# Loads that give each partition two neighbouring tokens, in a gated recurrence with an FFN behind it

## The chip, the cores and the metric

The kernel runs on one core of a Trainium2 chip. The core has five engines that run beside each other: TensorE (PE, matrix products; its weight loads are listed as PEld), VectorE (DVE), ScalarE (ACT), GpSimd (POOL) and SyncE (SP, which here only issues transfers). They share an on-chip memory of 128 partitions (SBUF), a smaller one for matmul results (PSUM) and 16 DMA engines. The metric is the device time of one execution in microseconds, and lower is better. The median of three runs of the kernel before is 515.47 us (515.06 to 516.38).

## What is computed

The input is a batch of 4 sequences of 5824 tokens with 256 channels. A gated linear recurrence runs over each sequence, and its output goes through a feed-forward network with a product in the middle.

```python
log_a = c * sigmoid(r_gate) * log(clip(sigmoid(a_param)))   # c = 8
a_t   = exp(log_a)
x_gated = sqrt(max(1 - a_t * a_t, 1e-6)) * sigmoid(i_gate) * x
h = a_t[:, t] * h + x_gated[:, t]      # for t = 0 .. S-1; y[:, t] = h
a, b = y @ w1, y @ w2                  # 256 -> 1024
out = ((a * b) @ w3) @ w_out           # 1024 -> 1024 -> 256
```

## The kernel before

The 23,296 tokens are cut into 47 chunks: two of 256 tokens, 44 of 512, and one of 256 at the end. The recurrence runs along time, so it needs channels on the partitions and tokens along the free dimension, while the inputs lie in DRAM with tokens as rows. Each chunk therefore goes through these steps (the letters are those of the written order):

- `r`, `i`, `x` (`load`, L133): SP loads the three inputs with tokens on the partitions. Chunks in both sets `TURN_R` and `TURN_U` (0 to 4 and 7, `long_rows`) give each partition neighbouring tokens, in one run of 2 or 4 KB. All others give partition p the tokens p, p + 128, p + 256 and p + 384 of the chunk, in runs of 1 KB.
- `R`, `I`: ACT takes tanh of both gates. `p`, `t` (L159, L178): mostly POOL, adds one and multiplies with x.
- `V`, `U`: the results are turned so that channels lie on the partitions. Chunks in `TURN_R` (for V) or `TURN_U` (for U) are turned by TensorE into PSUM (tile `ptr`), all others by a transposing DMA into SBUF (tiles `rt` and `ut`). The turned tile holds the 128 tokens of the first slot, then those of the second, and so on.
- `d` (`decay`, L200): ACT takes the exponential into `a_t`, in order of time. `s` squares it, on POOL, ACT or DVE; `q` takes the root on ACT.
- `g` (`gated`, L224): DVE computes max(n, 1e-3) times the turned gated input, in place in `nrm`. For long rows it walks the PSUM tile with a step of 128 elements, so that `nrm` is in order of time.
- `h` (L249): DVE runs the recurrence as two scans, one for each 128 channels. `y`: POOL casts the state to bfloat16.
- `a`, `b` (L268): TensorE multiplies with `w1` and `w2`. `c` (L282 on DVE, L284 on ACT): the first product is copied out of PSUM. `m` (L296): DVE multiplies it with the second, which it reads from PSUM.
- `D` (L307): TensorE multiplies with the product of `w3` and `w_out`, which is formed once at the start. `e`, `o`: the result is copied out and stored.

The order of all these steps is one list written out by hand (`ORDER`). Each engine works through its own part of that list in order and waits on semaphores for what it needs from the others. The gate steps of a chunk stand several chunks ahead of its FFN steps. Buffers are rings of a fixed length (`RINGS`): 4 one-bank PSUM tiles `po` for the first products, the turns and the results, 2 two-bank tiles `pb` for the second products, 3 `sa` and 3 `g`.

Of the kernel before, what the change touches and what calls it, by code (L numbers as in the profile page):

```python
# [13 lines left out]
ALU = mybir.AluOpType  # L14
# [8 lines left out]
def kernel(  # L23
# [12 lines left out]
    nc = tc.nc  # L36
    P = 128
# [11 lines left out]
    CT = 512  # L49
    sizes = [256, 256] + [CT] * 44 + [256]  # L50
    assert sum(sizes) == NTOK
    NCH = len(sizes)
    starts = [sum(sizes[:c]) for c in range(NCH)]
# [24 lines left out]
    T = {}  # L78
# [27 lines left out]
    def ring(pool, shape, dtype, name, tag):  # L106
        slot = taken[tag] % RINGS[tag]
        taken[tag] += 1
        return pool.tile(shape, dtype, name=name, tag=f"{tag}_{slot}")

    src = {"r": rf, "i": jf, "x": xf}
# [12 lines left out]
    def long_rows(c):  # L124
        return c in TURN_R and c in TURN_U

    def turned(t):
        return t.rearrange("p (j q) -> p q j", q=P)

    def in_time(t):  # L130
        return t.rearrange("p (q j) -> p q j", q=P)

    def load(c, nm):  # L133
        n = sizes[c] // P
        t = ring(loads, [P, 4, D], F32, name=nm + "_t", tag=nm)
        nc.sync.dma_start(  # L136
            out=t[:, :n, :],
            in_=src[nm][starts[c]:starts[c] + sizes[c], :].rearrange("(p n) c -> p n c" if long_rows(c) else "(n p) c -> p n c", p=P))
        T[nm, c] = t

    def tanh_r(c):
# [58 lines left out]
    def decay(c, cb):  # L200
        w = sizes[c]
        if cb == 0:
            T["a", c] = ring(held, [P, NCB, CT], F32, name="a_t", tag="a")
        a, pr = T["a", c][:, cb, :w], T["pr", c][:, cb, :w]
        if long_rows(c):
            a, pr = in_time(a), turned(pr)
        nc.scalar.activation(out=a, in_=pr, func=AF.Exp, scale=la4[:, cb:cb + 1], bias=la4[:, cb:cb + 1])  # L207

    def square(c, cb):
# [14 lines left out]
    def gated(c):  # L224
        w = sizes[c]
        if long_rows(c):
            for cb in range(NCB):
                n = in_time(T["n", c][:, cb, :w])
                nc.vector.scalar_tensor_tensor(out=n, in0=n, scalar=1e-3, in1=turned(T["pu", c][:, cb, :w]),
                                               op0=ALU.max, op1=ALU.mult)  # L230
            return
        nc.vector.scalar_tensor_tensor(  # L232
            out=T["n", c][:, :, :w], in0=T["n", c][:, :, :w], scalar=1e-3,
            in1=T["pu", c][:, :, :w], op0=ALU.max, op1=ALU.mult)

    def scan(c, cb):
        w = sizes[c]
# [179 lines left out]
    def last(c):  # L417
        return c == NCH - 1

    steps = {  # L420
        "r": lambda c: load(c, "r"), "i": lambda c: load(c, "i"), "x": lambda c: load(c, "x"),
        "R": tanh_r, "I": tanh_i, "p": plus, "t": times,
        "V": lambda c: turn_pe(c, "pr", "thr") if c in TURN_R else turn_dma(c, "pr", "thr"),
        "U": lambda c: turn_pe(c, "pu", "u") if c in TURN_U else turn_dma(c, "pu", "u"),
        "d": decay, "s": square, "q": root, "g": gated, "h": scan, "y": cast,
        "a": up_a, "b": up_b,
        "c": copy, "m": product, "D": down,
# [181 lines left out]
```

## Time and profile before

| What | Value |
|---|---|
| Median of three runs | 515.47 us (515.06 to 516.38) |
| Profiled execution | span 513.8 us from the first to the last instruction; no other time is listed for it |
| Granted clock of TensorE | 1.00 |
| DMA packets | 177,281, of these 86,354 under 512 B |
| Loads r, i, x of 512 KB | 44 each, median 5.3, 5.9 and 5.9 us from issue to landing |
| Turns by DMA | 40 of r, 39 of u, median 4.4 us |
| HBM read and written | 78.91 and 23.86 MB |

The page lists the busy time of each engine and its share of the span, a row of digits for each engine (its busy tenths in 40 equal slices of the span), the waits, and groups of instructions by line. In a group, the numbers behind the first bar are the total busy time in us and the mean of one instruction in ns; those behind the second are the idle time of the engine just before these instructions and what ended it. A wait is read as "who, at which line, waited for whom: us in total, times, longest". In the timeline a row begins with its start and its length in us. Several instructions of one kind in a row are merged, so a length can be that of two.

### The profile page before, as it was taken

The numbers are of one execution on the slowest core, as the hardware profiler recorded it, in microseconds if no ns is written. First come the engines' busy times: TensorE is split into PE (matmuls) and PEld (weight loads), VectorE is DVE, ScalarE is ACT, GpSimd is POOL, SyncE is SP. The second block draws the span as 40 slices with busy tenths as digits, with TensorE's granted clock in tenths as the row PEclk, the third lists the DMA queues.
The fourth block names the chain that finished last, engine by engine and source line by source line (L and its number), as shares of the span: only waits on it lengthen the run. The fifth ranks groups of instructions, "written<-read, shape, count | busy, mean of one in ns | idle before, by whom it ended". The sixth has DMA issues, their size and how long they took to land.

```text
span 513.8 us, 9036 instructions
## 1 busy us (share of the span) xinstructions
PE 499.8 (97%) x3267; PEld 314.2 (61%) x3321; DVE 430.6 (84%) x414; ACT 465.5 (91%) x720; POOL 312.9 (61%) x271
## 2 busy tenths in 40 slices
PE   7889999999999999999999999999999999999997
PEld 7658565566565566556656556564566655656566
DVE  5889999999999889978878799888878697959762
ACT  8899999999999999999999999998998979888543
POOL 2583858646637956866595983957646569480200
PEclk9999999999999999999999999999999999999999
DMA  8997999999989998896999996989795995252112
GB/s 299 410 414 255 305 315 285 312 240 316 314 242 269 266 276 261 221 276 201 289 288 310 262 272 191 234 228 246 197 265 132 215 316 170 101 150 76 54 60 103
DMA packets 177281, 123.82 MB, mean 241 GB/s; under 512 B 86354, under 2 KB 172884, under 8 KB 177236
## 3 DMA queue, kind: packets, MB, share of 16 engines
q1 hardware_dynamic: 177232, 123.23, 84.6%
q8 instruction: 26, 0.43, 0.3%
q14 instruction: 19, 0.16, 0.1%
q10 hardware_dynamic: 4, 0.00, 0.0%
HBM read 78.91 MB, written 23.86 MB: 200 GB/s over the span
## 4 chain that ended last, share of the span: by engine, by line
PE 86%; ACT 5%; DMA 4%; issue 2%; DVE 2%; SPq 1%; ACTq 0%; DVEq 0%
PE po L307 29%; PE pb L268 28%; PE pa L268 27%; DMA r_t<-in_r_gate_dram 4%; ACT sa L284 2%; PE pw L378 1%; PE ptr L185 1%; DVE g_t L296 1%; PE ptw L367 1%; ACT ot L284 1%; SPq L136 1%; DVE h_t L249 1%; ACT i_t L154 1%; ACT a_t L207 1%; ACT L154 0%
## 5 line engine op out<-in xcount | busy, mean ns | idle before, releaser
L296 DVE TENSOR_TENSOR g_t<-sa,pb 128x1024 bf16<-128x1024 bf16 (+1 forms) x188 | 219.0, 1181 | 62.0 <-PE pb L268 29.1
L268 PEld LDWEIGHTS <-w_sb 128*128 128x128 bf16 x1504 | 146.3, 98 | 146.8 <-issue 5.5
L284 ACT CAST sa<-pa 128x512 bf16<-128x512 f32 (+1 forms) x339 | 182.4, 588 | 27.6 <-PE pa L268 18.3
L268 PE MATMUL pa<-y_t,w_sb 128*128 128x512 bf16 (+1 forms) x721 | 185.9, 372 | 4.5 <-ACT sa L284 3.5
L268 PE MATMUL pb<-y_t,w_sb 128*128 128x512 bf16 (+1 forms) x729 | 182.5, 372 | 1.5
L307 PE MATMUL po<-wp_sb,g_t 128*128 128x256 bf16 x1456 | 177.7, 273 | 0.4
L307 PEld LDWEIGHTS <-g_t 128*128 128x128 bf16 x1456 | 142.4, 98 | 40.5 <-issue 0.9
L258 POOL CAST y_t<-h_t 128x1024 bf16<-128x1024 f32 (+1 forms) x46 | 51.2, 1112 | 141.2 <-DVE h_t L249 138.8
L178 POOL TENSOR_TENSOR u_t<-i_t,x_t 128x512 bf16<-128x512 f32 (+1 forms) x89 | 120.0, 1365 | 5.5 <-DMA ut<-u_t 2.5
L249 DVE TENSOR_TENSOR_SCAN h_t<-a_t,h_t,nrm 128x512 f32<-128x512 f32 (+1 forms) x92 | 121.0, 1345 | 1.9
L217 POOL TENSOR_TENSOR nrm<-a_t 128x512 f32<-128x512 f32 (+1 forms) x74 | 81.3, 1116 | 12.8 <-ACT a_t L207 9.9
L207 ACT ACTIVATE a_t<-rt,la 128x512 f32<-128x512 bf16 (+1 forms) x80 | 64.2, 821 | 0.0
L159 POOL TENSOR_SCALAR i_t<-i_t 128x1024 f32<-128x1024 f32 (+1 forms) x45 | 53.4, 1189 | 17.6 <-ACT i_t L154 17.6
L284 ACT COPY ot<-po 128x512 f32<-128x512 f32 (+1 forms) x85 | 49.6, 590 | 11.8 <-PE po L307 11.5
L232 DVE SCALAR_TENSOR_TENSOR nrm<-nrm,ut 128x1024 f32<-128x1024 f32 (+1 forms) x39 | 54.4, 1394 | 5.2 <-ACT nrm L221 5.2
L154 ACT ACTIVATE i_t<-i_t 128x1024 f32<-128x1024 f32 (+1 forms) x47 | 49.2, 1049 | 0.1
L221 ACT ACTIVATE nrm<-nrm 128x1024 f32<-128x1024 f32 (+1 forms) x47 | 48.4, 1040 | 0.2
L147 ACT ACTIVATE th_r<-r_t 128x1024 bf16<-128x1024 f32 (+1 forms) x40 | 42.6, 1065 | 0.0
L282 DVE CAST sa<-pa 128x512 bf16<-128x512 f32 (+1 forms) x37 | 21.9, 617 | 1.4 <-PE pa L268 1.1
L221 ACT ACT_TABLE_LOAD x17 | 21.8, 1283 | 0.4
L215 ACT ACTIVATE nrm<-a_t 128x512 f32<-128x512 f32 (+1 forms) x17 | 10.7, 648 | 0.1
L263 PE MATMUL warm<-ident 128*128 128x128 bf16 x128 | 10.2, 247 | 0.0
(57 smaller groups left out, 132.6 us busy)
## 6 DMA issues: line engine op xcount, KB each, us to landing
out_dram<-ot SPq DMA_DIRECT2D x90, 256.0 KB, 3.4
r_t<-in_r_gate_dram SPq DMA_DIRECT2D x44, 512.0 KB, 5.3
i_t<-in_i_gate_dram SPq DMA_DIRECT2D x44, 512.0 KB, 5.9
x_t<-in_x_dram SPq DMA_DIRECT2D x44, 512.0 KB, 5.9
wf<-in_moe_w_dram SPq DMA_DIRECT2D x12, 512.0 KB, 10.1
wf<-in_moe_w_out_dram SPq DMA_DIRECT2D x2, 512.0 KB, 10.5
r_t<-in_r_gate_dram SPq DMA_DIRECT2D x3, 256.0 KB, 2.7
i_t<-in_i_gate_dram SPq DMA_DIRECT2D x3, 256.0 KB, 3.8
```

The source lines that it names most:

```text
L154: nc.scalar.activation(out=t[:, :n, :], in_=t[:, :n, :], func=AF.Tanh, scale=0.5)
L159: (nc.vector if c in DV_PLUS else nc.gpsimd).tensor_scalar(t, t, 1.0, 1.0, op0=ALU.add, op1=ALU.mult)
L178: (nc.vector if (c, half) in DV_HALF else nc.gpsimd).tensor_mul(out=u, in0=t, in1=xt)
L207: nc.scalar.activation(out=a, in_=pr, func=AF.Exp, scale=la4[:, cb:cb + 1], bias=la4[:, cb:cb + 1])
L217: (nc.vector if (c, cb) in DV_SQUARE else nc.gpsimd).tensor_mul(out=n, in0=a, in1=a)
L221: nc.scalar.activation(out=T["n", c][:, :, :w], in_=T["n", c][:, :, :w], func=AF.Sqrt, scale=-1.0, bias=1.0)
L232: nc.vector.scalar_tensor_tensor(out=T["n", c][:, :, :w], in0=T["n", c][:, :, :w], scalar=1e-3, in1=T["pu", c][:, :, :w], op0=ALU.max, op1 ...
L249: nc.vector.tensor_tensor_scan(h[:, cb, :], a[:, cb, :], n[:, cb, :], init, ALU.mult, ALU.add)
L268: nc.tensor.matmul(out=dst[:, :w], lhsT=w_sb[:, cb, m * P:(m + 1) * P], rhs=T["y", c][:, cb, :w], start=(cb == 0), stop=(cb == NCB - 1))
L284: nc.scalar.copy(out=dst, in_=src_ps)
L296: nc.vector.tensor_mul(out=T["g", c][:, 2 * mp:2 * mp + 2, :w], in0=T["sa", c, mp][:, :, :w], in1=T["pb", c, mp][:, :, :w])
L307: nc.tensor.matmul(out=po, lhsT=T["g", c][:, k, j * P:(j + 1) * P], rhs=wp_sb[:, k, :], start=(k == 0), stop=(k == KD - 1), skip_group_che ...
```

## The change

Chunks that are not `long_rows` now give partition p the tokens 2p and 2p + 1 of each 256 tokens, one run of 2 KB, instead of single tokens 128 apart. After the turn, the 128 even tokens of a 256-token block lie in front of its 128 odd ones. Two steps put them back in order of time as they write or walk the float32 tile with a step of two elements: the exponential, which stays one instruction for each 128 channels, and the gated input, which becomes two instructions, one for the even and one for the odd tokens. The scans, the squares and all that follows read tiles in order of time as before. Loads of long rows, and the steps behind them, keep their form.

```diff
+    def run(c):
+        return sizes[c] // P if long_rows(c) else 2
+
+    def paired(t):
+        return t.rearrange("p (h q j) -> p h j q", q=P, j=2)
+
+    def halves(t):
+        return t.rearrange("p (h j q) -> p h j q", q=P, j=2)
+
 ...
         nc.sync.dma_start(
-            out=t[:, :n, :],
-            in_=src[nm][starts[c]:starts[c] + sizes[c], :].rearrange("(p n) c -> p n c" if long_rows(c) else "(n p) c -> p n c", p=P))
+            out=t[:, :n, :].rearrange("p (h j) c -> p h j c", j=run(c)),
+            in_=src[nm][starts[c]:starts[c] + sizes[c], :].rearrange("(h p j) c -> p h j c", p=P, j=run(c)))
 ...
         if long_rows(c):
             a, pr = in_time(a), turned(pr)
+        else:
+            a, pr = paired(a), halves(pr)
         nc.scalar.activation(out=a, in_=pr, func=AF.Exp, scale=la4[:, cb:cb + 1], bias=la4[:, cb:cb + 1])
 ...
-        nc.vector.scalar_tensor_tensor(
-            out=T["n", c][:, :, :w], in0=T["n", c][:, :, :w], scalar=1e-3,
-            in1=T["pu", c][:, :, :w], op0=ALU.max, op1=ALU.mult)
+        for j in range(2):
+            if w == CT:
+                n = T["n", c].rearrange("p cb (x j) -> p j (cb x)", j=2)[:, j].rearrange("p (y q) -> p y q", q=P)
+                pu = T["pu", c].rearrange("p cb (h j q) -> p j (cb h) q", q=P, j=2)[:, j]
+            else:
+                n = T["n", c][:, :, :w].rearrange("p cb (q j) -> p j cb q", j=2)[:, j]
+                pu = T["pu", c][:, :, :w].rearrange("p cb (j q) -> p j cb q", q=P)[:, j]
+            nc.vector.scalar_tensor_tensor(out=n, in0=n, scalar=1e-3, in1=pu, op0=ALU.max, op1=ALU.mult)
```

## The prediction

> **What bounds the kernel now.** I read the page's busy times and slices first, then the waits by engine, then groups by form, then the timeline around single instructions.
>
> ```profile
> PE 499.8 (97%) x3267; PEld 314.2 (61%) x3321; DVE 430.6 (84%) x414; ACT 465.5 (91%) x720; POOL 312.9 (61%) x271
> ...
> PE   7889999999999999999999999999999999999997
> ...
> DVE  5889999999999889978878799888878697959762
> ACT  8899999999999999999999999998998979888543
> ```
>
> A busy PE is not yet PE at its peak, so I compared the starts of neighbouring matmuls: 512 columns take 216 ns and 256 take 109 ns nearly everywhere from 28 us to 511 us. The gaps beyond that are mostly of one matmul's length, the mark of missing records. TensorE sets the end and has perhaps 1 us to give back after the start-up. VectorE and ScalarE run close beside it:
>
> ```profile
> 55.00:100.00 45.00, 44.70 (x294) 27.61 (x298) 43.83 (x47) 44.82 (x65) 32.22 (x30) 1.00 1.12 301
> 250.00:300.00 50.00, 49.74 (x305) 30.13 (x309) 40.88 (x32) 48.92 (x77) 39.37 (x32) 1.00 1.06 285
> ```
>
> (The columns are the stretch, its length, busy us of PE, weight loads, DVE, ACT and POOL, clock, DMA share, GB/s.) ACT is 98 to 99% busy until 350 us; DVE falls from 97% to between 82 and 90%. The waits tell who is late for whom:
>
> ```profile
> PE pa L268 <- ACT sa L284: 3.5, 3, 2.2
> PE ptr L185 <- ACT th_r L145: 2.2, 2, 1.2
> ...
> DVE g_t L296 <- PE pb L268: 29.1, 35, 2.7
> DVE g_t L296 <- ACT sa L284: 19.9, 25, 2.4
> ```
>
> PE hardly waits for anybody, and DVE's largest wait is for PE. So removing work elsewhere gains nothing; adding work costs only where it uses up the lead that DVE and ACT have over PE.
>
> **What the Trainium skill says.** "SBUF — State Buffer", section "SBUF: two separate sides", says that GpSimd shares a port pair with VectorE under an exclusive lock: a VectorE operation with two SBUF inputs and a GpSimd operation that reads SBUF exclude each other for a whole instruction. The trace agrees. The gated input is such an operation:
>
> ```profile
> 181.34 2.50 POOL L178 TENSOR_TENSOR u_t<-i_t,x_t 128x512 bf16<-128x512 f32 x2 [0.98 <-DMA ut<-u_t]
> 182.65 2.28 DVE L232 SCALAR_TENSOR_TENSOR nrm<-nrm,ut 128x1024 f32<-128x1024 f32 x1 [1.24 <-ACT nrm L221]
> ...
> 445.15 3.19 DVE L249 TENSOR_TENSOR_SCAN h_t<-a_t,h_t,nrm 128x512 f32<-128x512 f32 x2
> ...
> 445.57 1.69 POOL L217 TENSOR_TENSOR nrm<-a_t 128x512 f32<-128x512 f32 x1 [0.30 <-ACT a_t L207]
> ```
>
> At 182.65 the gated input took 2.28 us instead of its usual 1.22 because POOL's product had started 0.08 us before it. At 445 two scans follow each other without a gap, and POOL asked in the middle of the first. POOL got the ports between the two, and the second scan took 2.00 us instead of 1.26. This is the pattern that matters below.
>
> "SBUF — State Buffer", section "Specifications (TRN2)", gives 16-byte lines with at least two accesses per line needed for full bandwidth. A step of two float32 is 8 bytes, two accesses per line, so just inside. No instruction of this trace steps through SBUF element by element, so it neither agrees nor disagrees. "VectorE: DVE Perf Modes", section "Walkthrough: the 8-slice pipeline in each mode", says that the one-element-a-cycle mode takes any stride. The gated input runs at that rate: (1222 - 680)/512 = 1.06 ns an element.
>
> **The change, part by part.** All durations are of the profiled execution (span 513.8 us). The median of the runs is 515.47, 1.67 us above that span, and I add differences to the median.
>
> *Loads.* Chunks 5, 6 and 8 to 45 have three loads of 512 KB each, and chunk 46 three of 256 KB. Their 1 KB packets become half as many 2 KB packets. In the packet records a 1 KB packet takes 46 ns and a 2 KB packet 84 ns (medians), so 62,208 x 46 / 16 = 179 us of each DMA engine become 31,104 x 84 / 16 = 163 us, 16 us less. After the start-up only POOL is listed as waiting for a load, three times, 3.1 us in all, and POOL is busy for 61%. The loads of chunks 0 to 4 and 7, which are waited for at the start, keep their form. Worth nothing, then; SP issues as many transfers in the same order.
>
> *Decay.* The 82 Exp instructions of those chunks write float32 with a step of two. Neither their number nor their place changes. The long-row form (strided read from PSUM, contiguous write) took 784 ns against 773 for the contiguous one from the same source, so a strided read costs 1%; a strided write isn't shown. At best it costs nothing; at worst the part that grows with size doubles, which is 2 x (827 - 600) = 454 ns by the rows of 512 and 256 elements, +37 us of ACT. I take zero, by the 16-byte lines.
>
> *Gated input.* One instruction over 1024 becomes two over 512, 41 instructions more on DVE.
>
> ```profile
> L249 DVE TENSOR_TENSOR_SCAN h_t<-a_t,h_t,nrm 128x512 f32<-128x512 f32 x88 | 118.1, 1372 | 1.9
> ...
> L207 ACT ACTIVATE a_t<-rt,la 128x512 f32<-128x512 bf16 x78 | 63.1, 827 | 0.0
> L232 DVE SCALAR_TENSOR_TENSOR nrm<-nrm,ut 128x1024 f32<-128x1024 f32 x38 | 53.7, 1412 | 5.2 <-ACT nrm L221 5.2
> ...
> L229 DVE SCALAR_TENSOR_TENSOR nrm<-nrm,ptr 128x512 f32<-128x512 f32 x8 | 5.1, 680 | 0.0
> ```
>
> Undisturbed the whole took 1222 ns (the median of L232) and a half takes 680 (L229, the same operation). That is 2 x 680 - 1222 = 138 ns for each of 40 chunks, 5.5 us, and 0.1 us for chunk 46.
>
> Then the lock. In 14 of the 38 cases that read SBUF, a POOL instruction came while the whole gated input held the ports, and had to wait to its end. In 13 of them it came in the first half. With two instructions that POOL operation takes the ports between the halves, as between the scans at 445 us, and the second half waits for it: five casts of 1.036 us, three squares of 1.037, four products of 1.27, one addition of 1.04, together 14.4 us. DVE gets 5.6 + 14.4 = 20 us longer, to about 450 of 514 us. Behind the second half on DVE stand the two scans of the chunk and the products of the FFN, and PE waits for the products, which free its pb buffers.
>
> How much of 20 us reaches PE? pb has two buffers. From the trace I took, for every pair of up-projections after the first, the time from the end of the product that frees its buffer to PE's first weight load for it: between 130 and 430 us the median is 1.23 us and the lower quarter 0.71 us. A product that is late by 138 ns costs PE 0.008 us on average over this distribution, and one late by 138 + 1100, 0.31 us. If DVE stays late over two products, the worse of two costs 0.014 and 0.52 us. So 27 chunks give 0.2 to 0.4 us and the 13 with a collision 4.1 to 6.7 us: 4.3 to 7.1 us. I take 5.2, a little below the middle, since DVE's waits of about 1.7 us per chunk (45.1 us idle between 150 and 450 us, 26 chunks) absorb part of what stays late. Forecast: 515.5 + 5.2 = 520.7 us.
>
> The new waits are harmless: the built program gives POOL's addition on the tanh (L159) a wait for the load, which its input had to pass already. PE, ACT, POOL and SP keep their instructions in number and order.
>
> **The rivals.** *Hidden* (chance 0.14): POOL does not get in between the halves, because the second is issued 84 ns before the first ends and keeps the ports. Then only 5.6 us of DVE work are added, in pieces of 138 ns against leads of which 7% are smaller: 0.2 to 0.5 us, 515.8 us, not slower. It decides if collisions in the second halves stay under three or so (3 x 0.4 = 1.2 us). For it: of 33 back-to-back pairs of scans found, only one second scan was disturbed. Against it: in that one POOL had asked, and won.
>
> *Strided writes cost* (0.17): if the step of two slows ACT's write or DVE's read and write, the engines beside PE become the bound. ACT has 1 to 2% idle until 350 us, and 200 ns more on each of 82 Exps is 16 us of ACT. About half shows, since ACT has 10% to spare after 350 us: +8 us on top of +5, 529 us. If DVE's halves doubled, they would take 2 x 540 ns x 40 = 43 us more, and DVE would need 493 of 514 us: 540 us or more. The 8-byte step against the 16-byte lines speaks against it; no row of the trace does.
>
> *Faster* (0.04): the lighter DMA brings the turned tiles sooner. DMA share is over 1.0 from 55 to 150 us, but PE and ACT wait for no transfer there; POOL's 2.5 us of waiting for ut is the one place. PE itself has 1 us to win: 514.5 us.
>
> **How the numbers follow.** The main case has 0.65 and its own range of 517 to 524. Below it lie the hidden and the faster case, above it strided writes. To leave out 2 in 10, I cut near the middle of the hidden case and within the strided one, where ScalarE alone is slowed: 515.8 to 529. About 0.3%, 1.5 us, is what a measurement can tell from no change. The hidden case falls within that; the main and the strided case lie above it: faster 0.04, same 0.14, slower 0.82.
>
> **What would show it.** In the profile after: 80 halves of 512 in place of 40 wholes, with a minimum near 680 ns and a mean near 900 or more, some of them over 1.6 us beside a POOL instruction that started in the half before; DVE near 450 us; Exp still at 820 ns; more than 3.5 us in which PE waits for DVE's products or ACT's copies; 2 KB packets and a lower DMA share without effect. A half of 1.2 us beside no POOL instruction, or an Exp over 900 ns, would show that strides cost. Halves of 680 throughout with a time unchanged would make the lock, and the prediction, wrong.

## The result and the profile after

The changed kernel takes 521.12 us (median of 4 runs, 520.61 to 521.88), the kernel before 515.9 us beside it. The ratio is 1.0099, with a 95% interval of 1.0078 to 1.012. It is slower by 5.2 us; the forecast was also 5.2 us, on a median of 515.5 us for the kernel before, which made 520.7 us.

The profiled execution has a span of 518.8 us. Its page gives these busy times, and of the slices the rows of the three engines that were shown before:

```profile
PE 501.7 (97%) x3267; PEld 313.9 (61%) x3321; DVE 443.1 (85%) x455; ACT 468.4 (90%) x720; POOL 310.2 (60%) x271
...
PE   7799999999999999999999999999999999999997
...
DVE  4899999999999879989979699988989698859762
ACT  6999999999998999999999999998997969888553
...
PE 71%; ACT 10%; DVE 8%; DMA 5%; issue 4%; SPq 0%; ACTq 0%; DVEq 0%
```

DVE has 41 instructions more and is busy for 12.5 us longer, ACT for 2.9 us longer with the same 720 instructions. The last line is the chain that ended last. In the kernel before it was:

```profile
PE 86%; ACT 5%; DMA 4%; issue 2%; DVE 2%; SPq 1%; ACTq 0%; DVEq 0%
```

DVE went from 2 to 8% of it, and ACT from 5 to 10%. The stretches that were shown of the kernel before, and one from late in the run, show where PE is less busy (columns: stretch, length, busy us of PE, weight loads, DVE, ACT, POOL, then clock, DMA share and GB/s):

```profile
55.00:100.00 45.00, 44.45 (x294) 27.69 (x298) 43.79 (x50) 44.82 (x63) 32.14 (x30) 1.00 1.09 299
...
250.00:300.00 50.00, 49.19 (x306) 30.20 (x310) 41.31 (x37) 48.60 (x77) 39.21 (x32) 1.00 1.01 286
...
400.00:450.00 50.00, 48.75 (x302) 29.88 (x306) 40.30 (x38) 43.40 (x69) 30.07 (x25) 1.00 0.79 215
```

From 400 to 450 us PE is busy for 48.75 us; before it was 49.68:

```profile
400.00:450.00 50.00, 49.68 (x311) 30.81 (x315) 41.76 (x35) 44.51 (x70) 32.69 (x26) 1.00 0.70 196
```

The waits name a releaser that PE never had before, in the first line:

```profile
PE pb L284 <- DVE g_t L312: 2.6, 5, 0.9
...
PE pa L284 <- ACT sa L300: 2.2, 3, 1.1
...
DVE g_t L312 <- PE pb L284: 28.7, 32, 3.2
DVE g_t L312 <- ACT sa L300: 19.0, 27, 2.2
```

Five times PE waits for a product that frees a pb buffer, 2.6 us in all. The groups by form, with the total us and the mean ns of one behind the bar, show the two edited steps and the scans:

```profile
L265 DVE TENSOR_TENSOR_SCAN h_t<-a_t,h_t,nrm 128x512 f32<-128x512 f32 x88 | 115.7, 1345 | 1.9
...
L250 DVE SCALAR_TENSOR_TENSOR nrm<-nrm,ut 128x512 f32<-128x512 f32 x76 | 68.7, 945 | 5.6 <-ACT nrm L232 5.3 <-DMA ut<-u_t 0.2
...
L218 ACT ACTIVATE a_t<-rt,la 128x512 f32<-128x512 bf16 x78 | 66.6, 874 | 0.0
```

A half of the gated input takes 945 ns in the mean; its median is 693 ns, so most are undisturbed and some are far above. Exp went from 827 to 874 ns. One collision can be followed from POOL to PE in the timeline of all engines (start, length, instruction; a length with x2 covers two):

```profile
422.82 2.11 DVE L250 SCALAR_TENSOR_TENSOR nrm<-nrm,ut 128x512 f32<-128x512 f32 x2
423.04 1.34 POOL L274 CAST y_t<-h_t 128x1024 bf16<-128x1024 f32 x1 [4.59 <-DVE h_t L265]
...
424.86 2.34 DVE L312 TENSOR_TENSOR g_t<-sa,pb 128x1024 bf16<-128x1024 bf16 x2
```

and in that of PE alone:

```profile
424.16 1.03 PE L284 MATMUL pb<-y_t,w_sb 128*128 128x512 bf16 x4
426.12 1.02 PE L284 MATMUL pb<-y_t,w_sb 128*128 128x512 bf16 x4 [0.93 <-DVE g_t L312]
```

POOL's cast had waited for the last scan. It starts 0.22 us after the first half, gets the port pair that the two engines share when that half ends, and the second half waits behind it: the two halves take 685 and 1526 ns. So the product starts only at 424.86 and ends at about 426.1. The next pb needs the buffer that it frees, and PE stands for 0.93 us. In the kernel before, the same cast met a whole gated input at 419.06 us and was the one to wait.

### The profile page after: what moved, and what is told of

Read it like the earlier page. It is cut to its first block, busy times and chain, and to the rows that moved or that the text cites. A ratio compares the mean times of both kernels' runs of the same rounds, so it can differ in the third digit from the quotient of the medians.

```text
span 518.8 us, 9105 instructions
## 1 busy us (share of the span) xinstructions
PE 501.7 (97%) x3267; PEld 313.9 (61%) x3321; DVE 443.1 (85%) x455; ACT 468.4 (90%) x720; POOL 310.2 (60%) x271
## 2 busy tenths in 40 slices
DMA packets 146178, 123.82 MB, mean 239 GB/s; under 512 B 86355, under 2 KB 110677, under 8 KB 146133
## 3 DMA queue, kind: packets, MB, share of 16 engines
q1 hardware_dynamic: 146128, 123.23, 82.6%
## 4 chain that ended last, share of the span: by engine, by line
PE 71%; ACT 10%; DVE 8%; DMA 5%; issue 4%; SPq 0%; ACTq 0%; DVEq 0%
PE po L323 24%; PE pb L284 23%; PE pa L284 22%; DMA wf<-in_moe_w_dram 4%; ACT sa L300 4%; DVE g_t L312 3%; DVE nrm L250 3%; ACT a_t L218 2%; DVE h_t L265 2%; PE pw L394 1%; DMA x_t<-in_x_dram 1%; ACT nrm L232 1%; ACT i_t L163 1%; ACT ot L300 1%; ACT th_r L156 1%
## 5 line engine op out<-in xcount | busy, mean ns | idle before, releaser
L274 POOL CAST y_t<-h_t 128x1024 bf16<-128x1024 f32 (+1 forms) x46 | 49.0, 1064 | 149.0 <-DVE h_t L265 116.0
L187 POOL TENSOR_TENSOR u_t<-i_t,x_t 128x512 bf16<-128x512 f32 (+1 forms) x89 | 121.7, 1384 | 6.9 <-DMA ut<-u_t 3.7
L265 DVE TENSOR_TENSOR_SCAN h_t<-a_t,h_t,nrm 128x512 f32<-128x512 f32 (+1 forms) x92 | 118.6, 1318 | 1.9
L250 DVE SCALAR_TENSOR_TENSOR nrm<-nrm,ut 128x512 f32<-128x512 f32 (+1 forms) x78 | 69.4, 931 | 5.6 <-ACT nrm L232 5.3
L218 ACT ACTIVATE a_t<-rt,la 128x512 f32<-128x512 bf16 (+1 forms) x80 | 67.8, 868 | 0.0
L168 POOL TENSOR_SCALAR i_t<-i_t 128x1024 f32<-128x1024 f32 (+1 forms) x45 | 51.1, 1138 | 17.9 <-ACT i_t L163 17.9
```

The costliest lines, as they stand in the source:

```text
L168: (nc.vector if c in DV_PLUS else nc.gpsimd).tensor_scalar(t, t, 1.0, 1.0, op0=ALU.add, op1=ALU.mult)
L187: (nc.vector if (c, half) in DV_HALF else nc.gpsimd).tensor_mul(out=u, in0=t, in1=xt)
L265: nc.vector.tensor_tensor_scan(h[:, cb, :], a[:, cb, :], n[:, cb, :], init, ALU.mult, ALU.add)
```

## Where PE falls behind

PE runs all its instructions in one order in every kernel here, so the start of a chunk's first down-projection can be compared between traces. The table gives this start minus the same start in the kernel before. What chunk 0 shows stays the same up to chunk 4; its D comes before the first edited instruction of ACT or DVE, at 55.5 us.

| Start of D of chunk | 0 | 11 | 15 | 27 | 33 | 36 | 41 | 46 | 0 to 46 |
|---|---|---|---|---|---|---|---|---|---|
| in the kernel before, us | 48.5 | 152.8 | 191.9 | 321.6 | 387.9 | 409.2 | 461.7 | 508.7 | |
| changed | 0.63 | 1.15 | 2.08 | 2.91 | 3.33 | 3.91 | 4.89 | 5.03 | 4.40 |
| changed, second profile | 1.42 | 1.99 | 2.93 | 2.68 | 3.06 | 3.63 | 4.61 | 4.74 | 3.32 |
| split alone, contiguous | 1.22 | 1.24 | 1.95 | 2.54 | 2.88 | 3.46 | 3.40 | 3.41 | 2.19 |
| split undone | 0.03 | 0.70 | 0.65 | 0.48 | 0.73 | 0.73 | 0.73 | 0.73 | 0.70 |
| Exp's step undone | 0.43 | 0.53 | 1.43 | 1.44 | 1.75 | 2.32 | 3.30 | 3.43 | 3.00 |
| before, and a small multiplication | 1.96 | 2.12 | 3.15 | 3.30 | 3.87 | 4.43 | 5.34 | 5.41 | 3.45 |
| before, and a small sum | 0.37 | 0.42 | 0.38 | 0.01 | 0.01 | 0.01 | 0.26 | 0.32 | -0.05 |
| changed, nine halves apart | 1.51 | 2.07 | 3.01 | 3.94 | 4.53 | 5.11 | 6.09 | 6.22 | 4.71 |

The rows below the first two of the change belong to experiments that follow. The delay does not grow with the number of chunks but in a few steps, of 0.9 us near 155 us, 0.6 near 395 and 1.0 near 425, the last of which is the collision above. These three come just after the second halves of chunks 15, 37 and 40 were hit, and make 2.5 of the 4.4 us. The rest arose before chunk 11 and in steps of 0.65 and 0.35 us near 270 and 335 us, of which only the second stands in both profiles. The step before chunk 11 is another matter: it is there with the split undone and not without the slower Exp. The last column is what arose after the start-up. The first one is a spread between executions of work that no edit touches; where it was largest, the clock granted to TensorE between 28 and 49 us was 0.92 in place of 1.00. It is not a trait of some of these kernels: of 111 executions of the kernel before beside the experiments, 60 show a mean clock of 0.997 in place of 1.00, and of those with the small sum 17 of 22. What starts it is open.

## The experiments

The theory, called the opened lock in the expectations, was that the second half waits behind POOL for the ports, that the product behind it comes late, and that PE then waits. The rival was Exp: ACT is busy for 95% or more of each stretch from 55 to 350 us, and its strided write turned out slower. Ratios are to the kernel before in runs on the same chip.

**The split alone**, in contiguous halves, one for each 128 channels:

```diff
-        nc.vector.scalar_tensor_tensor(
-            out=T["n", c][:, :, :w], in0=T["n", c][:, :, :w], scalar=1e-3,
-            in1=T["pu", c][:, :, :w], op0=ALU.max, op1=ALU.mult)
+        for cb in range(NCB):
+            nc.vector.scalar_tensor_tensor(
+                out=T["n", c][:, cb, :w], in0=T["n", c][:, cb, :w], scalar=1e-3,
+                in1=T["pu", c][:, cb, :w], op0=ALU.max, op1=ALU.mult)
```

> The kernel before with one edit: the gated input of every chunk that is not long-row is two instructions over 512 contiguous elements, one for each 128 channels. Loads, Exp and the step of two stay out. Theory of the opened lock: about 13 second halves take over 1.5 us, DVE's busy time rises by about 11 us to 442, and the time rises by 3.5 to 5 us, most of the 5.2 us of the whole change. Rival, the slower Exp: less than 1.5 us, since ACT gets no more work here.

Measured: 1.0044 (1.003 to 1.0059), 2.3 us. Thirteen second halves were hit, between 1.52 and 1.76 us long, and DVE was busy for 439.9 us, so the mechanism is there, but the time is below what was expected. The traces show two differences from the changed kernel. One is a hit that did not happen. POOL's cast came 0.22 us into the first half of chunk 40, as at 422.82 us in the changed kernel, and this time the second half went first:

```profile
422.17 1.27 DVE L233 SCALAR_TENSOR_TENSOR nrm<-nrm,ut 128x512 f32<-128x512 f32 x2
422.39 1.95 POOL L259 CAST y_t<-h_t 128x1024 bf16<-128x1024 f32 x1 [4.63 <-DVE h_t L250]
```

The halves took 666 and 684 ns, and the step of 1.0 us near 425 us is missing in the table. In the seven traces with halves that stand together, POOL asked during a first half 81 times, and this is the only time that it did not get in between. Why it did not here is open.

The other difference is the scan, where it stands right behind the halves, in 17 chunks. It needs only the first of these two, and started 82 ns before the second ended; in the changed kernel it needs both and starts 104 ns after (medians of the 17 places). That gives back up to 0.19 us of DVE's time at each of them. What it is worth to PE was not measured by itself.

**Exp alone**, with its step of two, and nothing else:

```diff
         if long_rows(c):
             a, pr = in_time(a), turned(pr)
+        else:
+            a, pr = paired(a), halves(pr)
```

> The kernel before with one edit: Exp writes with the step of two (chunks that are not long-row). Loads and gated input stay as they were, so tokens in the decay tile stand in another order than the reference's; the work is the same. Exp should take 868 ns instead of 824, 3.5 us more on ACT. Theory of the opened lock: ACT's lead hides most of it, 0 to 1.5 us. Rival, the slower Exp: 3 us or more, as ACT is 98 to 99% busy until 350 us.

Measured: 1.0008 (0.9996 to 1.0021). Exp takes 874 ns. ACT's lead hides 3.5 us of added work, or all but a few tenths.

**The loads alone:**

```diff
-            out=t[:, :n, :],
-            in_=src[nm][starts[c]:starts[c] + sizes[c], :].rearrange("(p n) c -> p n c" if long_rows(c) else "(n p) c -> p n c", p=P))
+            out=t[:, :n, :].rearrange("p (h j) c -> p h j c", j=run(c)),
+            in_=src[nm][starts[c]:starts[c] + sizes[c], :].rearrange("(h p j) c -> p h j c", p=P, j=run(c)))
```

> The kernel before with one edit: the loads in 2 KB runs, with no step behind them that puts the tokens back, so tokens are processed in another order than the reference's; the work is the same. Both theories: no change within 0.3% (1.5 us), about 31,000 packets fewer, DMA time 2 to 3% of the span lower. A gain of over 1.5 us would mean that loads did bound something.

Measured: 1.0006 (0.9994 to 1.0017). The loads give and cost nothing.

**One more small instruction on DVE**, in the kernel before, behind each whole gated input:

```diff
+        nc.vector.tensor_scalar(zt, zd, 1.0, None, op0=ALU.mult)
```

> The kernel before with one addition: behind each whole gated input stands one more DVE instruction on two elements (about 165 ns, some 80 ns of DVE's time since neighbours overlap by 84 ns). It adds the occupancy of the split (2 x (680 - 84) against 1222 - 84, 54 ns) and a little more, but opens the ports nowhere for longer. Theory of the opened lock: 0 to 1 us slower. Rival, that any added DVE work costs: 3 us or more.

Measured: 1.0081 (1.0064 to 1.0097), 4.2 us for 41 multiplications of two elements each. The expectation missed, and the trace says why. The instruction's own line (shortest, median and longest in ns) and the place that was followed above, in this kernel:

```profile
L235 DVE TENSOR_SCALAR zt<-zd x41: 154/163/1236, 68.7 to 496.2; 128x2 f32<-128x2 f32 x41
```

```profile
423.28 1.20 DVE L232 SCALAR_TENSOR_TENSOR nrm<-nrm,ut 128x1024 f32<-128x1024 f32 x1
423.49 1.88 POOL L259 CAST y_t<-h_t 128x1024 bf16<-128x1024 f32 x1 [4.65 <-DVE h_t L250]
424.39 1.00 DVE L235 TENSOR_SCALAR zt<-zd 128x2 f32<-128x2 f32 x1
425.31 2.34 DVE L297 TENSOR_TENSOR g_t<-sa,pb 128x1024 bf16<-128x1024 bf16 x2
```

The small multiplication waits for the ports too. In 16 of 41 places it took 1.00 to 1.24 us, behind a POOL instruction that had been waiting for the gated input to end. The Trainium skill, "SBUF — State Buffer", section "SBUF: two separate sides", counts VectorE's modes with two ports among those that take the shared pair, next to operations with two inputs in SBUF, and the waits agree with that; in which mode the multiplication ran is not shown. So this run had not left out the suspected cause but had repeated it, with an instruction that needs almost no time of its own. It needed a counterpart that does not ask for the ports.

**A small sum in the same place:**

```diff
+        nc.vector.tensor_reduce(out=zt[:, :1], in_=zd, axis=mybir.AxisListType.X, op=ALU.add)
```

> The kernel before with one addition: behind each whole gated input one sum over two elements on DVE (about 160 ns). The multiplication of two elements in the same place cost 1.0081 and waited 16 times for about 1 us behind POOL. If that wait was the cost and the sum[...] does not wait for POOL: no instance over 300 ns, time within 0.25% of the kernel before. If one more DVE instruction is enough by itself: 1.005 or more. If the sum waits for POOL as well, it repeats the 1.008 and tells nothing new.

Measured: 1.0012 (1.0003 to 1.0022), 0.6 us. No instance waited (shortest, median, longest), and at the same collision the sum goes through while POOL holds the ports:

```profile
L235 DVE TENSOR_REDUCE zt<-zd x41: 140/142/149, 67.1 to 491.1; 128x1 f32<-128x2 f32 x41
```

```profile
418.84 1.20 DVE L232 SCALAR_TENSOR_TENSOR nrm<-nrm,ut 128x1024 f32<-128x1024 f32 x1
419.06 1.88 POOL L259 CAST y_t<-h_t 128x1024 bf16<-128x1024 f32 x1 [4.64 <-DVE h_t L250]
...
419.96 0.15 DVE L235 TENSOR_REDUCE zt<-zd 128x1 f32<-128x2 f32 x1
```

The two kernels have the same number of DVE instructions in the same places, of nearly the same length when undisturbed. One costs 0.81%, the other 0.12%. They are different operations, but what the traces show to differ is the waiting: the multiplication has to get the ports after POOL has asked for them, and the sum does not. So one more DVE instruction costs little by itself, and one that waits for POOL costs most of what the change does.

**The split undone**, loads and Exp left as changed:

```diff
-        for j in range(2):
...
-            nc.vector.scalar_tensor_tensor(out=n, in0=n, scalar=1e-3, in1=pu, op0=ALU.max, op1=ALU.mult)
+        nc.vector.scalar_tensor_tensor(
+            out=T["n", c][:, :, :w], in0=T["n", c][:, :, :w], scalar=1e-3,
+            in1=T["pu", c][:, :, :w], op0=ALU.max, op1=ALU.mult)
```

> The changed kernel with one part undone: the gated input is one whole instruction again. Loads of 2 KB and Exp with the step of two stay, so the gated input is multiplied with tokens in another order than the reference's. Theory of the opened lock: 515.5 to 517 us, at most 1.5 us over the kernel before. Rival, the slower Exp: 519 us or more.

Measured: 1.0011 (1.0002 to 1.0021). Without the split some 0.6 us are left of 5.2.

**Where Exp's 47 ns come from.** The same three dimensions, contiguous inside:

```diff
+    def blocks(t):
+        return t.rearrange("p (h j q) -> p j h q", q=P, j=2)
 ...
+        elif w == CT:
+            a, pr = blocks(a), blocks(pr)
```

> The kernel before with one edit: Exp walks its four blocks of 128 elements in another order, on both sides, so that it has the same three dimensions as in the changed kernel but no step of two. If the 44 ns more of Exp come from the step of two on the write, Exp stays at about 824 ns here; if they come from the extra dimensions, it takes about 868 ns. Time within 1.5 us of the kernel before in either case.

Measured: 0.9998 (0.9985 to 1.0011). The groups by form of this kernel and of the one with Exp's step alone:

```profile
L212 ACT ACTIVATE a_t<-rt,la 128x512 f32<-128x512 bf16 x78 | 63.1, 828 | 0.0
```

```profile
L215 ACT ACTIVATE a_t<-rt,la 128x512 f32<-128x512 bf16 x78 | 66.5, 874 | 0.0
```

It is the step of two on the write, not the dimensions.

**The changed kernel again, and with one more part undone each:** the loads back to 1 KB, and Exp back to its contiguous write. The edits are the reverse of the last two diffs of loads and Exp.

> The changed kernel once more, on the chip of the next three, so that they can be set against it. Expected 1.008 to 1.012 times the kernel before.

> The changed kernel with the loads as before (1 KB runs); Exp with the step of two and the split gated input stay, so the tokens stand in another order than the reference's. The split alone gave 1.0044 and loads with Exp 1.0011, the whole 1.0099. If the slower Exp makes the delays of the split count more, this stays near 1.009 to 1.010. If the loads in 2 KB do, it falls to about 1.005.

> The changed kernel with Exp as before (contiguous write); loads of 2 KB and the split gated input stay, so the tokens of the decay tile stand in another order than the reference's. If the slower Exp makes the delays of the split count more: about 1.005, Exp back at 824 to 828 ns. If it doesn't: 1.008 or more.

Measured: 1.0088 (1.0074 to 1.0103) for the changed kernel, 1.0091 (1.0072 to 1.011) without its loads, 1.0071 (1.0052 to 1.009) without Exp's step. The loads are out of it. Without Exp's step the ratio falls by 0.0017, some 0.9 us, and the two intervals overlap; by the table Exp is worth 0.3 to 1.4 us after the start-up. The 1.0071 lies between the two values that had been expected, so Exp does not explain the whole gap to the contiguous split alone. In the traces the gap is 1.1 to 2.2 us after the start-up, and 1.0 us of it is the hit near 422 us that the contiguous split escaped.

**Halves apart.** The first half is moved in front of the DVE instruction before it, in 29 chunks, and then in the 9 of them that this list names with the product:

```diff
+    AHEAD = {19: 'm16.2', 25: 'm22.3', 26: 'm23.3', 28: 'm26.0', 32: 'm29.0',
+             31: 'm28.3', 33: 'm30.3', 34: 'm32.1', 35: 'm33.1'}
 ...
-        for j in range(2):
+        for j in js:
 ...
+    for c, product_word in AHEAD.items():
+        words.insert(words.index(product_word), f"G{c}")
```

> The changed kernel with the first half of the gated input moved in front of the DVE instruction before it, in 29 of 41 chunks; that instruction reads one operand from PSUM and never waited for the ports. POOL can then use the ports while that instruction runs. Theory of the opened lock: fewer second halves over 1.2 us (14 before, 6 or fewer now), DVE's busy time down by some 8 us, 1.004 to 1.007 times the kernel before. Rival, that the sheer number of DVE instructions costs: 1.009 or more, no change.

> As the run with halves apart, but only in 9 chunks (19, 25, 26, 28 and 31 to 35) whose second half was hit by POOL in the changed kernel and where the earlier first half met no long wait for its root. All 29 moves together cost more than they gave, with DVE's waits for the root of ACT up from 5.2 to 12.9 us. Theory of the opened lock: those waits stay near 5 to 6 us, DVE is busy for some 6 us less, and the time falls below the changed kernel's 1.0088 to about 1.006 to 1.0075. If moving the halves costs by itself (the products behind them come later), it is 1.009 or more.

Measured: 1.0164 (1.0143 to 1.0185) and 1.0106 (1.0079 to 1.0132). In the first, DVE stands for the root of ACT for 12.9 us in place of 5.3, with the products behind it:

```profile
DVE nrm L251 <- ACT nrm L233: 12.9, 7, 4.1
```

In the second that wait stays at 5.3 us and only 5 of the halves that still stand together were hit. The groups by form show the shorter halves, and the page the shorter busy time:

```profile
L251 DVE SCALAR_TENSOR_TENSOR nrm<-nrm,ut 128x512 f32<-128x512 f32 x76 | 62.9, 860 | 6.4 <-ACT nrm L233 5.3 <-ACT th_r L157 0.7 <-DMA ut<-u_t 0.4
```

```profile
PE 505.7 (97%) x3321; PEld 315.5 (61%) x3321; DVE 436.7 (84%) x455; ACT 468.3 (90%) x720; POOL 312.8 (60%) x271
```

DVE got back 6.4 us of its 12.5, as forecast, and the kernel did not get faster. The trace shows two reasons. First, the hits that PE had felt most were not among the nine. The halves of chunks 15, 37 and 40 stayed together and were hit again (1526, 1758 and 1526 ns), and the steps of the delay near 155, 395 and 425 us are as large as in the changed kernel (0.96, 0.58 and 0.98 us). The nine hits that the list takes on stand beside only 0.4 to 1.0 us of the delay there. Second, a half that goes first delays the product that it was moved past. For chunk 19 it can be followed:

```profile
199.52 1.46 DVE L251 SCALAR_TENSOR_TENSOR nrm<-nrm,ut 128x512 f32<-128x512 f32 x1
...
202.14 1.07 ACT L301 CAST sa<-pa 128x512 bf16<-128x512 f32 x2 [1.09 <-DVE g_t L313]
202.78 1.02 PE L285 MATMUL pa<-y_t,w_sb 128*128 128x512 bf16 x4 [0.99 <-ACT sa L301]
```

The moved half itself waits for POOL and takes 1.46 us, the product behind it starts only at 200.90 us, ACT waits 1.09 us for that product, and PE 0.99 us for ACT's copy. That fits the theory, in that a late product costs and a busy DVE does not, but it refutes the step from fewer hits to less time: it matters which product is late. Whether sparing the three hits that matter would help was not tried, and this is no remedy. No kernel here beats the one before.

## Why the prediction was right

**What bounds the kernel.** Right. PE was saturated and had nothing to win; no edit made the kernel measurably faster.

**Loads.** Right: packets fell from 177,281 to 146,178, DMA time from 84.6 to 82.6% of 16 engines' span, the time not at all.

**Exp.** The step "I take zero, by the 16-byte lines" was wrong. The write with a step of 8 bytes costs 47 ns of 827, 3.5 us on ACT. The Trainium skill, "SBUF — State Buffer", section "Specifications (TRN2)", asks for two accesses per line, which this write has, and yet it is slower; the measurement decides. Exp at 874 ns lies between the 820 that was expected and the 900 that was to show that strides cost. Far below the rival's 200 ns more, it costs the kernel some 0.4 to 0.9 us by the medians of the two experiments, of which the first cannot be told from nothing; by the table it is mostly lost before chunk 11. That ACT is 98 to 99% busy until 350 us was not quite so: from 150 to 200 us it was 95%.

**The fixed cost of the split.** Mis-sized: 138 ns a chunk, from 2 x 680 - 1222. Neighbours on DVE overlap by 84 ns, and one more instruction has one more overlap, so it is 54 ns, 2.2 us in place of 5.5. An undisturbed half with `ut` from SBUF took 684 ns in the mean against 682 when contiguous: for DVE the step is free here.

**The collisions.** Right in mechanism and number: 13 were forecast from POOL instructions that had come in the first half of a whole, and 14 second halves were hit, all 13 among them. Together they took 12.8 us more than 680 ns each, in place of 14.4.

**DVE's busy time.** Forecast 450 us, measured 443.1. Of the 20 us, 3.3 fall to the overlap and 1.6 to the size of the hits; the scans took 2.4 us less in all, with 14 of them over 1.3 us in place of 16.

**What reaches PE.** The range of 4.3 to 7.1 us was for the split alone. The split undone leaves about 0.6 us, so the split takes about 4.6 of 5.2, at the lower end. That the point forecast of 5.2 us was met is luck: Exp, which had been taken at zero, adds what the split falls short. The reckoning with one distribution of leads gave every collision 0.31 to 0.52 us. In the trace most cost PE little, and three of the 14 stand behind 2.5 us.

**The rivals.** *Hidden* is excluded: it allowed three or so hits, there were 14, and the split undone takes most of the time back. The one second half that kept the ports, in the contiguous split, shows that what it supposed can happen. *Strided writes cost* was true of ACT at a quarter of its assumed size. *Faster* was not seen.

## What to carry to other kernels

Splitting a VectorE instruction that needs the ports it shares with GpSimd is not priced by its two durations. Ask what GpSimd has waiting while the whole instruction runs: such an instruction got in between the halves in 80 of 81 cases here, and all that stands behind the second half on VectorE was then late by about its full length. Take the waits in the trace of before as the collisions of after; all 13 came true here. Then judge each by the lead that the results behind it have at that place, and not by the busy time of the engine or by an average: three of 14 collisions made most of the loss, and sparing nine others gained nothing.

## What was not expected of the hardware

A VectorE multiplication of two elements in SBUF waited 16 times in 41 for 0.8 to 1.1 us behind GpSimd, while a sum over two elements in the same place never did (140 to 149 ns). ScalarE's Exp with a float32 write in steps of 8 bytes took 874 ns in place of 827, and VectorE's gated input in the same steps lost nothing. Two instructions on VectorE that follow each other without a wait overlap by 84 ns, and a scan that had to wait for the one right before it started 104 ns after its end in 12 of 17 places and 35 ns after in five, a difference of up to 0.19 us for each such pair. GpSimd, which had asked during the first of two such instructions, got the ports before the second in 80 of 81 cases, though the second starts 84 ns before the first ends.
